# Five gate/up tiles in token halves that share a PSUM bank, a split block 0 down projection and new scheduler estimates, in a fused state-space and gated-MLP kernel

## The chip, the cores and the metric

The kernel runs on one core of a Trainium2 chip. The metric is device time in microseconds (us) of one execution. PE is TensorE, PEld its weight loads, DVE VectorE, ACT ScalarE, SP the engine that issues the DMAs. "L717" is line 717 of the kernel in question; the changed kernel has more lines, so the same statement has another number there.

## The reference, cut to what matters

```python
xn = layernorm(x)                                   # x: 2048 tokens x 512, bf16
A  = 2*Re(C @ scan(Lam_bar, B_bar @ xn)) + xn*Dskip # 512 complex states, scanned over tokens
B  = (gelu(xn @ w_gate) * (xn @ w_up)) @ w_down     # hidden size 1376
out = x + A + B
```

## The kernel before

The tokens are cut into 4 blocks of 512, and each block into 4 token tiles of 128. The hidden size is cut into 11 tiles ("ft"). For each block PE does gate/up (`GU`, 8 matmuls of 512 columns per hidden tile), the B projection of the scan (`BU`, 32 matmuls) and the down projection joined with the C projection (`DN`, 19 matmuls per token tile: 11 hidden parts, 8 state parts). The order on PE and SP is the program's. The order on DVE, ACT and POOL comes from a list scheduler, run when the kernel is built, which works with estimated durations:

```python
def d_pe(n_list):                                   # estimate of matmuls of n columns, ns
    return sum(max(n / 2.4 + 2.5, 64.0 + n / 4.7) for n in n_list)
```

At the start the normalized tokens of block 0 are transposed on PE and copied out of PSUM (where the results of PE land, in banks of 512 columns) by DVE or ACT, and three hidden tiles begin before all four token tiles are there:

```python
def TR0(j, eng):          # 4 transposes of token tile j, then a copy on DVE ("V") or ACT ("A")
    ...
def GU(b, fts=None, halves=False):
    ...
    if halves:
        for ft in fts:
            banks[ft] = (next_bank(), next_bank())          # gate bank, up bank
        def part(W, Wc, i, j0, j1):
            for ft in fts:
                mm(ft, W, Wc, banks[ft][i], 128 * j0, 128 * j1, XT0[j0:j1])
        part(WG, WGc, 0, 0, 1)      # gate, token tile 0: 12 matmuls of 128 columns
        part(WG, WGc, 0, 1, 2)      # gate, token tile 1
        part(WU, WUc, 1, 0, 2)      # up, token tiles 0 and 1: 12 of 256 columns
        TR0(2, "V")
        TR0(3, "A")
        part(WG, WGc, 0, 2, 3)
        part(WG, WGc, 0, 3, 4)
        part(WU, WUc, 1, 2, 4)
    for ft in fts:
        ...                         # other tiles: 8 matmuls of 512 columns
        # gelu (ACT) of the gate bank, copy (ACT) of the up bank, product (DVE)
```

```python
# order of the program (cut)
LN(0, [0, 1], True); TR0(0, "V"); TR0(1, "A"); fill(4); params()   # 4 filler matmuls
LN(0, [2, 3], True); load_B()
GU(0, [0, 1, 2], halves=True); tables_dve(); GU(0, [3, 4])
BU(0); CHAIN(0, 2); ...; GU(0, range(5, KF)); BU(1); ...
BU(2); CHAIN(2); DN(0); ...; DN(3)
```

`params()` puts some small operations on DVE (four to sixteen columns each). The weights come in three chunks each (hidden tiles 0 to 2, 3 to 6, 7 to 10); SP issues x tiles, gate chunk 0, up chunk 0, gate chunk 1, up chunk 1, and later the B transposes and chunk 2. Before all that, 11 warm-up matmuls run on PE.

Of the kernel before, what the change touches and what calls it, by code (L numbers as in the profile page):

```python
# [9 lines left out]
ALU = mybir.AluOpType  # L10
ACTF = mybir.ActivationFunctionType
# [2 lines left out]
ENGINES = ("tensor", "vector", "scalar", "gpsimd", "sync")  # L14
SYNC_LAT = 120.0
SELF_LAT = 40.0
DMA_ISSUE = 500.0
INORDER = ("tensor", "sync")

# [55 lines left out]
class Sched:  # L75
# [88 lines left out]
    def _backward(self, span):  # L164
        ops = self.ops
        left = {op.id: len(op.users) for op in ops}
        late = {op.id: span for op in ops}
        ready = {e: [] for e in ENGINES}
        last = {e: [op for op in ops if op.eng == e] for e in INORDER}
        for op in ops:  # L170
            if left[op.id] == 0 and op.eng not in INORDER:
                ready[op.eng].append(op)
        busy = {e: span for e in ENGINES}
        begin = {}
        n = len(ops)
        while n:
            best = None
            for e in ENGINES:
                if e in INORDER:
                    if not last[e] or left[last[e][-1].id]:  # L180
                        continue
                    op = last[e][-1]
                else:
                    if not ready[e]:
                        continue
                    op = max(ready[e], key=lambda o: (min(busy[e], late[o.id]), o.finish, o.id))
                end = late[op.id] if op.kind == "dma" else min(busy[e], late[op.id])
                if best is None or end > best[0]:
                    best = (end, op)
            end, op = best  # L190
            e = op.eng
            if e in INORDER:
                last[e].pop()
            else:
                ready[e].remove(op)
            begin[op.id] = end - op.dur
            if op.kind == "dma":
                begin[op.id] = min(begin[op.id], busy[e] - op.issue)
                busy[e] = begin[op.id]
            else:  # L200
                busy[e] = begin[op.id]
            n -= 1
            for d in op.deps:
                late[d.id] = min(late[d.id], begin[op.id] - (SELF_LAT if d.eng == op.eng and d.kind == "eng" else SYNC_LAT))
                left[d.id] -= 1
                if left[d.id] == 0 and d.eng not in INORDER:
                    ready[d.eng].append(d)
        return begin

    def _forward(self, prio):  # L210
        ops = self.ops
# [10 lines left out]
        nleft = len(ops)  # L222

        def rdy_time(op):
            return max([d.finish + (SELF_LAT if d.eng == op.eng and d.kind == "eng" else SYNC_LAT) for d in op.deps], default=0.0)

        while nleft:
            best = None
            for e in ENGINES:
                if e in INORDER:  # L230
                    if qpos[e] >= len(queue[e]):
                        continue
                    op = queue[e][qpos[e]]
# [3 lines left out]
                else:  # L237
# [4 lines left out]
                    stb, b = min(cands, key=lambda c: (prio[c[1].id], c[1].id))  # L242
# [107 lines left out]
EPS_BF16 = 1.0013580322265625e-05  # L350

def d_pe(n_list):
    return sum(max(n / 2.4 + 2.5, 64.0 + n / 4.7) for n in n_list)
def d_dve_tt2x(n): return 100.0 + 0.52 * n
def d_dve_1x(n): return 100.0 + 1.04 * n
def d_dve_scan(n): return 90.0 + 2.08 * n
# [2 lines left out]
def d_act(n, ptr=0): return 190.0 + 0.833 * n + 90.0 * ptr  # L359
# [3 lines left out]
def build(nc, ins, out):  # L363
    with ExitStack() as es:
# [151 lines left out]
        def next_bank():  # L516
            b_ = rstate["n"] % 8
            rstate["n"] += 1
            return b_
# [21 lines left out]

        w16 = lambda a, b_: W16.ap[:, a:b_]
        W16p = [A.sub(A.alloc("W16v", [4, 4], F32, at=W16.lo), "W16_%d" % i, i) for i in range(4)]
        GATE = {"before_gelu": []}
        sinT, sinP, cosT, cosP = (SC16.ap[:, 4 * i:4 * i + 4] for i in range(4))
        def coefs():
            V(lambda e: e.tensor_tensor(pa(LBR), pa(RRr), cosT, ALU.mult), D_TINY, [PA[RRr], SC16], [PA[LBR]])
# [155 lines left out]
            V(lambda e: e.tensor_tensor(ssb.ap[:, :, 1, :], TB.ap[:, :, 0, :], TA.ap[:, :, 1, :], ALU.subtract),  # L703
              d_dve_tt2x(2048), [TA, TB], [SSc[k3][s][1] for s in range(KP)], "post_im")

        def GU(b, fts=None, halves=False):
            k2 = b % 2
            fts = list(range(KF) if fts is None else fts)
            banks = {}

            def mm(ft, W, Wc, bank, c0, c1, rd):
                m = FROWS[ft]

                def f(e):
                    ins_ = None
                    for dk in range(KD):
                        ins_ = e.matmul(PS[bank][0:m, c0:c1], W.ap[:, dk, 128 * ft:128 * ft + m], XNT[b].ap[:, dk, c0:c1],  # L717
                                        start=(dk == 0), stop=(dk == KD - 1))
                    return ins_
                PE(f, d_pe([c1 - c0] * 4), [Wc[wchunk(ft)]] + rd, [BANK[bank]], "GU%d" % b)  # L720

            if halves:
                for ft in fts:
                    banks[ft] = (next_bank(), next_bank())
                def part(W, Wc, i, j0, j1):
                    for ft in fts:
                        mm(ft, W, Wc, banks[ft][i], 128 * j0, 128 * j1, XT0[j0:j1])
                part(WG, WGc, 0, 0, 1)
                part(WG, WGc, 0, 1, 2)
                part(WU, WUc, 1, 0, 2)  # L730
                TR0(2, "V")
                TR0(3, "A")
                part(WG, WGc, 0, 2, 3)
                part(WG, WGc, 0, 3, 4)
                part(WU, WUc, 1, 2, 4)
            for ft in fts:
                m = FROWS[ft]
                if not halves:
                    banks[ft] = (next_bank(), next_bank())
                bg, bu = banks[ft]  # L740
                kk = (KF * b + ft) % 3
                if not halves:
                    for (W, Wc, bank) in zip((WG, WU), (WGc, WUc), banks[ft]):
                        mm(ft, W, Wc, bank, 0, 512, XTr(b))
                GATE["last_gelu"] = ACT(lambda e, bg=bg, kk=kk, m=m: e.activation(  # L745
                    GG[kk].ap[0:m, :], PS[bg][0:m, :], ACTF.Gelu_apprx_tanh),
                    d_act(512), [BANK[bg]], [GG[kk]], "gelu", after=GATE["before_gelu"])
                ACT(lambda e, bu=bu, kk=kk, m=m: e.activation(UPB[kk].ap[0:m, :], PS[bu][0:m, :], ACTF.Copy),  # L748
                    d_act(512), [BANK[bu]], [UPB[kk]], "evU")
                V(lambda e, kk=kk, m=m, ft=ft, k2=k2: e.tensor_tensor(  # L750
                    HTt[k2][ft].ap[0:m, :], GG[kk].ap[0:m, :], UPB[kk].ap[0:m, :], ALU.mult),
                  d_dve_tt2x(512), [GG[kk], UPB[kk]], [HTt[k2][ft]], "hmul")

        def DN(b):
            k2, k3 = b % 2, b % 3
            for j in range(4):
                tt = 4 * b + j
                bank = next_bank()
                ko = tt % 4
                ACT(lambda e, bank=bank, tt=tt: e.activation(PS[bank][:, :], X[tt].ap, ACTF.Copy),  # L760
                    d_act(512), [X[tt]], [BANK[bank]], "seed")

                def f(e, bank=bank, j=j, k2=k2, k3=k3, b=b):
                    mms = []
                    for ft in range(KF):
                        m = FROWS[ft]
                        mms.append((PS[bank][:, :], HTt[k2][ft].ap[0:m, 128 * j:128 * (j + 1)], WD.ap[0:m, ft, :]))
                    for s in range(KP):
                        for c in range(2):
                            mms.append((PS[bank][:, :], SSc[k3][s][c].ap[:, 128 * j:128 * (j + 1)], CT[c][s].ap))  # L770
                    ins_ = None
                    for n, (o_, l_, r_) in enumerate(mms):
                        ins_ = e.matmul(o_, l_, r_, start=False, stop=(n == len(mms) - 1), skip_group_check=True)  # L773
                    return ins_
                rds = [HTt[k2][ft] for ft in range(KF)] + WDc
                rds += [SSs[k3][s] for s in range(KP)] + [CT[c][s] for c in range(2) for s in range(KP)]
                PE(f, d_pe([512] * (KF + 8)), rds + [BANK[bank]], [BANK[bank]], "DN%d" % b)
                V(lambda e, bank=bank, ko=ko, tt=tt: e.tensor_tensor(OUTB[ko].ap, PS[bank][:, :], XD[tt].ap, ALU.add),  # L778
                  d_dve_1x(512), [BANK[bank], XD[tt]], [OUTB[ko]], "evO")
                S.dma(lambda e, tt=tt, ko=ko: e.dma_start(out[0, 128 * tt:128 * (tt + 1), :], OUTB[ko].ap),  # L780
                      128 * 1024, reads=[OUTB[ko]], is_output=True, tag="st_out")

        nwarm = 11
        wrm4 = WRM.ap.unsqueeze(1).broadcast_to([128, 4, 128])
# [20 lines left out]
        params()  # L805
        LN(0, [2, 3], True)
        load_B()
        GU(0, [0, 1, 2], halves=True)
        tables_dve()
        GU(0, [3, 4])  # L810
        GATE["before_gelu"] = [tables_act([GATE["last_gelu"]])]
        BU(0)
        CHAIN(0, 2)
# [11 lines left out]
        GU(1, range(0, 8)); TR(2); GU(1, range(8, KF))  # L825
        BU(2)
        CHAIN(2)
        DN(0)
        LN(3); SKIP(3)
        GU(2, range(0, 8)); TR(3); GU(2, range(8, KF))  # L830
        BU(3)
# [62 lines left out]
```

## Time and profile before

| | before |
|---|---|
| time, median of 3 runs | 182.54 us (182.50 to 182.59) |
| span of the profiled run | 180.8 us |
| first gate matmul | 6.84 us |
| transposes of token tiles 2 and 3 | 9.49 us |
| next gate matmul | 10.82 us |
| first B matmul | 16.93 us |

The page of the kernel before, part 1 (busy time, share of the span, instructions) and the first line of part 4 (the chain of waits that ended last):

```profile
PE 175.2 (97%) x848; PEld 82.8 (46%) x864; DVE 155.8 (86%) x264; ACT 92.0 (51%) x158; POOL 7.5 (4%) x19
...
PE 95%; DVE 2%; issue 1%; ACT 0%; DVEq 0%
```

PE is the bound. How near to its limit it is cannot be read from busy time, because a matmul's recorded end is modelled (the Trainium skill, "Perfetto Trace Analysis", Tensor Engine Instruction, calls it an estimate; here a 512-column matmul is recorded as 379 ns while the next one starts 216 ns after it). So I go by the distance of starts. It is 216 ns for 512 columns, 109 for 256 and 56 for 128, from 10.82 us to the end, except where a record is missing.

The timeline of the kernel before, PE alone (start us, length us, line, shape, count, idle time before and its releaser):

```profile
5.80 0.72 PE L629 MATMUL PS<-arena 128*128 128x128 bf16 x8
6.36 0.39 PE L796 MATMUL PS<-arena 128*128 128x128 bf16 x4
...
6.84 2.81 PE L717 MATMUL PS<-arena 128*128 128x128 bf16 x36
9.49 0.61 PE L629 MATMUL PS<-arena 128*128 128x128 bf16 x8
10.82 6.28 PE L717 MATMUL PS<-arena 128*128 128x128 bf16 x51 [0.72 <-DVE arena L637]
16.93 0.38 PE L654 MATMUL PS<-arena 128*128 128x512 bf16 x1
```

The last transpose starts at 9.88 us, the next matmul 937 ns later, where 56 would do: 0.88 us are lost. DVE releases it. The timeline of the kernel before, DVE and then ACT, around the wait:

```profile
9.71 0.18 DVE L539 CAST arena<-arena 128x16 int32<-128x16 f32 x1
9.92 0.17 DVE L540 TENSOR_TENSOR arena<-arena 128x16 f32<-128x16 f32 x1
10.01 0.15 DVE L534 TENSOR_TENSOR arena<-arena 128x4 f32<-128x4 bf16 x1
10.08 0.15 DVE L552 TENSOR_TENSOR arena<-arena 128x4 f32<-128x4 f32 x1
10.27 0.18 DVE L553 RECIPROCAL arena<-arena 128x4 f32<-128x4 f32 x1
10.37 0.39 DVE L637 COPY arena<-PS 128x512 bf16<-128x512 bf16 x1
```

```profile
10.13 0.60 ACT L635 ACTIVATE arena<-PS 128x512 bf16<-128x512 bf16 x1 [2.06 <-PE PS L629]
```

L637 is the copy of token tile 2 on DVE. ACT copies tile 3 as soon as PE has transposed it. The chain of the kernel before, in order of time (start, length, what), runs through that copy:

```profile
10.45 0.32 DVE arena L637
10.77 0.05 issue
10.82 2.82 PE PS L717 x36
```

### The profile page before, as it was taken

To read this page: it belongs to the slowest core of one execution; us is meant where nothing else is said; L and a number is where in the kernel's file an instruction comes from. 1 tells how busy PE (TensorE), PEld (TensorE's weight loads), DVE (VectorE), ACT (ScalarE), POOL (GpSimd) and SP (SyncE) were. 2 spreads that over 40 slices of the span, in tenths; PEclk is the share of its full clock that TensorE was granted. 3 is DMA by queue.
4 is the path that set the end of the run, shared out by engine and by line. 5 is a ranking of instruction groups with operands and counts; after the bars stand their busy time and mean duration, and the time that the engine had idled before them with its cause. 6 is when DMAs were issued, how large, how long until landed. Compare 5 with 4: busy or idle time off the path is not lost.

```text
span 180.8 us, 2356 instructions
## 1 busy us (share of the span) xinstructions
PE 175.2 (97%) x848; PEld 82.8 (46%) x864; DVE 155.8 (86%) x264; ACT 92.0 (51%) x158; POOL 7.5 (4%) x19
## 2 busy tenths in 40 slices
PE   7989999999999999999999999999999999999993
PEld 2674444444444444444444444444444444444441
DVE  4899679999999996999999999999989999982111
ACT  3378999776767997002667793000667700800000
POOL 2220202000000002000000000000000000000000
PEclk9999999999999999999999999999999999999999
DMA  5999914999000000001610000000000000021100
GB/s 128 305 325 165 313 31 103 244 320 189 14 0 0 4 0 0 29 29 60 90 30 0 0 2 0 33 29 29 29 0 0 4 0 0 0 87 35 54 31 29
DMA packets 24068, 12.38 MB, mean 68 GB/s; under 512 B 15385, under 2 KB 24057, under 8 KB 24057
## 3 DMA queue, kind: packets, MB, share of 16 engines
q1 hardware_dynamic: 24032, 12.23, 28.2%
q8 instruction: 7, 0.11, 0.2%
q14 instruction: 5, 0.03, 0.1%
q10 hardware_dynamic: 24, 0.00, 0.0%
HBM read 6.46 MB, written 2.10 MB: 47 GB/s over the span
## 4 chain that ended last, share of the span: by engine, by line
PE 95%; DVE 2%; issue 1%; ACT 0%; DVEq 0%
PE PS L717 41%; PE PS L773 36%; PE PS L654 15%; PE PS L790 3%; DVE arena L637 0%; DVE arena L608 0%; DVE arena L778 0%; DVE arena L595 0%; PE PS L629 0%; ACT arena L599 0%; ACT arena L600 0%; DVE arena L539 0%; DVE arena L596 0%; DVE arena L538 0%; DVE arena L553 0%
## 5 line engine op out<-in xcount | busy, mean ns | idle before, releaser
L717 PE MATMUL PS<-arena 128*128 128x512 bf16 (+3 forms) x393 | 76.7, 353 | 1.1 <-DVE arena L637 0.7
L773 PE MATMUL PS<-arena 128*128 128x512 bf16 (+1 forms) x296 | 65.6, 379 | 0.4
L717 PEld LDWEIGHTS PS<-arena 128*128 128x128 bf16 (+1 forms) x400 | 37.8, 100 | 38.9 <-DVE arena L637 0.9
L745 ACT ACTIVATE arena<-PS 128x512 bf16<-128x512 f32 (+1 forms) x44 | 26.3, 599 | 49.1 <-PE PS L717 37.1
L773 PEld LDWEIGHTS PS<-arena 128*128 128x128 bf16 (+1 forms) x304 | 29.7, 98 | 36.0
L687 DVE TENSOR_TENSOR_SCAN arena<-arena 128x512 bf16<-128x512 f32 x32 | 38.6, 1251 | 0.0
L748 ACT ACTIVATE arena<-PS 128x512 bf16<-128x512 f32 (+1 forms) x44 | 26.3, 600 | 6.7 <-PE PS L717 6.6
L654 PE MATMUL PS<-arena 128*128 128x512 bf16 x127 | 28.2, 379 | 0.1
L778 DVE TENSOR_TENSOR arena<-PS,arena 128x512 bf16<-128x512 f32 x16 | 10.8, 684 | 15.5 <-PE PS L773 15.5
L654 PEld LDWEIGHTS PS<-arena 128*128 128x128 bf16 x128 | 12.5, 98 | 15.0
L658 ACT ACTIVATE arena<-PS 128x512 bf16<-128x512 f32 x32 | 17.8, 596 | 2.1 <-PE PS L654 2.1
L750 DVE TENSOR_TENSOR arena<-arena 128x512 bf16<-128x512 bf16 (+1 forms) x44 | 17.4, 415 | 0.8 <-ACT arena L748 0.8
L595 DVE BATCH_NORM_STATS2 arena<-arena 128x6 f32<-128x512 bf16 x16 | 10.2, 680 | 3.5 <-DMA arena<-in_A_x_dram 3.5
L760 ACT ACTIVATE PS<-arena 128x512 f32<-128x512 bf16 x16 | 9.4, 603 | 0.7
L674 DVE TENSOR_TENSOR arena<-arena 128x4096 bf16<-128x4096 bf16 (+1 forms) x5 | 9.3, 1859 | 0.0
L676 DVE TENSOR_TENSOR arena<-arena 128x4096 bf16<-128x4096 bf16 (+1 forms) x5 | 9.3, 1858 | 0.0
L699 DVE TENSOR_TENSOR arena<-arena 128x4096 bf16<-128x4096 bf16 x4 | 9.2, 2288 | 0.1
L700 DVE TENSOR_TENSOR arena<-arena 128x4096 bf16<-128x4096 bf16 x4 | 9.1, 2284 | 0.0
L608 DVE TENSOR_SCALAR arena<-arena 128x512 bf16<-128x512 bf16 x16 | 5.6, 409 | 0.3
L615 DVE TENSOR_TENSOR arena<-arena 128x512 bf16<-128x512 bf16 x16 | 5.8, 416 | 0.0
L790 PE MATMUL PS<-arena 128*128 128x512 bf16 x11 | 4.9, 632 | 1.0 <-DVE arena L508 1.0
L571 DVE SCALAR_TENSOR_TENSOR arena<-arena 128x512 bf16<-128x512 bf16 x8 | 5.6, 747 | 0.0
(75 smaller groups left out, 66.1 us busy)
## 6 DMA issues: line engine op xcount, KB each, us to landing
out_dram<-arena SPq DMA_DIRECT2D x16, 128.0 KB, 1.7
arena<-in_A_x_dram SPq DMA_DIRECT2D x3, 512.0 KB, 7.6
arena<-in_B_w_down_dram SPq DMA_DIRECT2D x1, 1280.0 KB, 8.2
arena<-in_A_x_dram SPq DMA_DIRECT2D x4, 128.0 KB, 2.2
arena<-in_B_w_gate_dram SPq DMA_DIRECT2D x1, 512.0 KB, 5.8
arena<-in_B_w_up_dram SPq DMA_DIRECT2D x1, 512.0 KB, 6.7
arena<-in_B_w_gate_dram SPq DMA_DIRECT2D x1, 480.0 KB, 4.6
arena<-in_B_w_up_dram SPq DMA_DIRECT2D x1, 480.0 KB, 6.0
```

The source lines that it names most:

```text
L595: V(lambda e, tt=tt: e.bn_stats(ST[tt].ap, X[tt].ap), d_dve_1x(512), [X[tt]], [ST[tt]], "bnst")
L654: ins_ = e.matmul(PS[bank][:, :], BBT[c][dk].ap[:, 128 * s:128 * (s + 1)], XNT[b].ap[:, dk, :], start=(dk == 0), stop=(dk == KD - 1))
L658: ACT(lambda e, bank=bank, k3=k3, s=s, c=c: e.activation(SSc[k3][s][c].ap, PS[bank][:, :], ACTF.Copy), d_act(512), [BANK[bank]], [SSc[k3][ ...
L687: V(lambda e, g=g, rb=rb, init=init: e.tensor_tensor_scan(g.ap, rb, g.ap, init, ALU.mult, ALU.add), d_dve_scan(512), [g, PA[RRr]] + ([CARc ...
L717: ins_ = e.matmul(PS[bank][0:m, c0:c1], W.ap[:, dk, 128 * ft:128 * ft + m], XNT[b].ap[:, dk, c0:c1], start=(dk == 0), stop=(dk == KD - 1))
L745: GATE["last_gelu"] = ACT(lambda e, bg=bg, kk=kk, m=m: e.activation(GG[kk].ap[0:m, :], PS[bg][0:m, :], ACTF.Gelu_apprx_tanh), d_act(512), ...
L748: ACT(lambda e, bu=bu, kk=kk, m=m: e.activation(UPB[kk].ap[0:m, :], PS[bu][0:m, :], ACTF.Copy), d_act(512), [BANK[bu]], [UPB[kk]], "evU")
L750: V(lambda e, kk=kk, m=m, ft=ft, k2=k2: e.tensor_tensor(HTt[k2][ft].ap[0:m, :], GG[kk].ap[0:m, :], UPB[kk].ap[0:m, :], ALU.mult), d_dve_tt ...
L760: ACT(lambda e, bank=bank, tt=tt: e.activation(PS[bank][:, :], X[tt].ap, ACTF.Copy), d_act(512), [X[tt]], [BANK[bank]], "seed")
L773: ins_ = e.matmul(o_, l_, r_, start=False, stop=(n == len(mms) - 1), skip_group_check=True)
L778: V(lambda e, bank=bank, ko=ko, tt=tt: e.tensor_tensor(OUTB[ko].ap, PS[bank][:, :], XD[tt].ap, ALU.add), d_dve_1x(512), [BANK[bank], XD[tt ...
L790: ins_ = e.matmul(PS[wb][:, :].rearrange("p (a b) -> p a b", a=4), WRM.ap, wrm4, start=True, stop=True)
```

## The change

The intent: let five hidden tiles begin with the first half of the tokens, so that more matmuls stand behind the transposes of tiles 2 and 3 while these are copied. The gate and up results of a token half (256 columns each) share one PSUM bank. In block 0's down projection all hidden parts come first, so that the state parts are wanted later. The scheduler's estimates change too.

```diff
+LAT = lambda d, op: SYNC_LAT if d.kind == "dma" or d.eng != op.eng else (0.0 if d.eng == "tensor" else SELF_LAT)
...                                  # used in both passes of the scheduler
 def d_pe(n_list):
-    return sum(max(n / 2.4 + 2.5, 64.0 + n / 4.7) for n in n_list)
+    return sum(n / 2.4 + 2.5 for n in n_list)
...
+        def GU_first(fts, early, single):
+            banks = [{ft: next_bank() for ft in fts} for h in range(2)]
+            ...     # mm: gate in columns 0-255 of the bank, up in 256-511; evac: gelu, copy, product of 256
+            for u in range(2):
+                for ft in early:
+                    mm(ft, u, 0, 1)          # gate, then up, token tile 0
+                ...
+            for ft in early:
+                for u in range(2):
+                    mm(ft, u, 1, 2)          # token tile 1
+                evac(ft, 0)
+            late = [ft for ft in fts if ft not in early]
+            mm(late[0], 0, 0, 2)
+            TR0(2, "V")
+            TR0(3, "A")
+            for ft in late[1:]:
+                mm(ft, 0, 0, 2)
+            for ft in late:
+                mm(ft, 1, 0, 2)
+                evac(ft, 0)
+            for ft in fts:
+                for u in range(2):
+                    mm(ft, u, 2, 4)
+                evac(ft, 1)
...
-        def DN(b):
+        def DN(b, split=False):
...
+            if split:
+                for j in range(4):
+                    seed(j); hidden(j)
+                for j in range(4):
+                    states(j); store(j)
...
-        GU(0, [0, 1, 2], halves=True)
+        GU_first(range(5), range(3), False)
         tables_dve()
-        GU(0, [3, 4])
...
-        DN(0)
+        DN(0, True)
```

Sharing a bank is sound. The Trainium skill ("PSUM — Partial Sum Buffer", The four PSUM rules) says that a group's first matmul clears the accumulate bits of the whole bank, so that two groups may not be open in one bank at once. Here each group of four matmuls is complete before the next starts in that bank.

More of the change, by code (lines that the diff above doesn't have):

```diff
@@ L203, in _backward @@
             for d in op.deps:
-                late[d.id] = min(late[d.id], begin[op.id] - (SELF_LAT if d.eng == op.eng and d.kind == "eng" else SYNC_LAT))
+                late[d.id] = min(late[d.id], begin[op.id] - LAT(d, op))
                 left[d.id] -= 1
@@ L224, in rdy_time @@
         def rdy_time(op):
-            return max([d.finish + (SELF_LAT if d.eng == op.eng and d.kind == "eng" else SYNC_LAT) for d in op.deps], default=0.0)
+            return max([d.finish + LAT(d, op) for d in op.deps], default=0.0)
         while nleft:
@@ L543, in build @@
         W16p = [A.sub(A.alloc("W16v", [4, 4], F32, at=W16.lo), "W16_%d" % i, i) for i in range(4)]
-        GATE = {"before_gelu": []}
+        GATE = {"before_gelu": [], "nh": 0}
         sinT, sinP, cosT, cosP = (SC16.ap[:, 4 * i:4 * i + 4] for i in range(4))
@@ L704, in CHAIN, with mm, f, evac @@
               d_dve_tt2x(2048), [TA, TB], [SSc[k3][s][1] for s in range(KP)], "post_im")
-        def GU(b, fts=None, halves=False):
+        def GU_first(fts, early, single):
+            banks = [{ft: next_bank() for ft in fts} for h in range(2)]
+            def mm(ft, u, j0, j1):
+                W, Wc = ((WG, WGc), (WU, WUc))[u]
+                h, q0 = j0 // 2, 256 * u + 128 * (j0 % 2)
+                bank = banks[h][ft]
+                def f(e):
+                    ins_ = None
+                    for dk in range(KD):
+                        ins_ = e.matmul(PS[bank][:, q0:q0 + 128 * (j1 - j0)], W.ap[:, dk, 128 * ft:128 * (ft + 1)],
+                                        XNT[0].ap[:, dk, 128 * j0:128 * j1], start=(dk == 0), stop=(dk == KD - 1))
+                    return ins_
+                PE(f, d_pe([128 * (j1 - j0)] * 4), [Wc[wchunk(ft)]] + XT0[j0:j1], [BANK[bank]], "GU0")
+            def evac(ft, h):
+                bank, c0 = banks[h][ft], 256 * h
+                GATE["nh"] = kk = (GATE["nh"] + 1) % 3
+                GATE["last_gelu"] = ACT(lambda e: e.activation(GG[kk].ap[:, 0:256], PS[bank][:, 0:256], ACTF.Gelu_apprx_tanh),
+                                        d_act(256), [BANK[bank]], [GG[kk]], "gelu")
+                ACT(lambda e: e.activation(UPB[kk].ap[:, 0:256], PS[bank][:, 256:512], ACTF.Copy),
+                    d_act(256), [BANK[bank]], [UPB[kk]], "evU")
+                V(lambda e: e.tensor_tensor(HTt[0][ft].ap[:, c0:c0 + 256], GG[kk].ap[:, 0:256], UPB[kk].ap[:, 0:256], ALU.mult),
+                  d_dve_tt2x(256), [GG[kk], UPB[kk]], [HTt[0][ft]], "hmul")
+            for u in range(2):
+                for ft in early:
+                    mm(ft, u, 0, 1)
+                if single and u == 0:
+                    TR0(1, "A")
+            for ft in early:
[15 more added lines that the diff above has]
+                evac(ft, 1)
@@ L707, in GU @@
+        def GU(b, fts=None):
             k2 = b % 2
@@ L720, in mm @@
                 PE(f, d_pe([c1 - c0] * 4), [Wc[wchunk(ft)]] + rd, [BANK[bank]], "GU%d" % b)
-            if halves:
-                for ft in fts:
-                    banks[ft] = (next_bank(), next_bank())
-                def part(W, Wc, i, j0, j1):
-                    for ft in fts:
-                        mm(ft, W, Wc, banks[ft][i], 128 * j0, 128 * j1, XT0[j0:j1])
-                part(WG, WGc, 0, 0, 1)
-                part(WG, WGc, 0, 1, 2)
-                part(WU, WUc, 1, 0, 2)
-                TR0(2, "V")
-                TR0(3, "A")
-                part(WG, WGc, 0, 2, 3)
-                part(WG, WGc, 0, 3, 4)
-                part(WU, WUc, 1, 2, 4)
             for ft in fts:
                 m = FROWS[ft]
-                if not halves:
-                    banks[ft] = (next_bank(), next_bank())
+                banks[ft] = (next_bank(), next_bank())
                 bg, bu = banks[ft]
                 kk = (KF * b + ft) % 3
-                if not halves:
-                    for (W, Wc, bank) in zip((WG, WU), (WGc, WUc), banks[ft]):
-                        mm(ft, W, Wc, bank, 0, 512, XTr(b))
+                for (W, Wc, bank) in zip((WG, WU), (WGc, WUc), banks[ft]):
+                    mm(ft, W, Wc, bank, 0, 512, XTr(b))
                 GATE["last_gelu"] = ACT(lambda e, bg=bg, kk=kk, m=m: e.activation(
@@ L752, in GU @@
                   d_dve_tt2x(512), [GG[kk], UPB[kk]], [HTt[k2][ft]], "hmul")
-        def DN(b):
+        def DN(b, split=False):
             k2, k3 = b % 2, b % 3
-            for j in range(4):
-                tt = 4 * b + j
-                bank = next_bank()
-                ko = tt % 4
-                ACT(lambda e, bank=bank, tt=tt: e.activation(PS[bank][:, :], X[tt].ap, ACTF.Copy),
-                    d_act(512), [X[tt]], [BANK[bank]], "seed")
-                def f(e, bank=bank, j=j, k2=k2, k3=k3, b=b):
-                    mms = []
-                    for ft in range(KF):
-                        m = FROWS[ft]
-                        mms.append((PS[bank][:, :], HTt[k2][ft].ap[0:m, 128 * j:128 * (j + 1)], WD.ap[0:m, ft, :]))
-                    for s in range(KP):
-                        for c in range(2):
-                            mms.append((PS[bank][:, :], SSc[k3][s][c].ap[:, 128 * j:128 * (j + 1)], CT[c][s].ap))
-                    ins_ = None
-                    for n, (o_, l_, r_) in enumerate(mms):
-                        ins_ = e.matmul(o_, l_, r_, start=False, stop=(n == len(mms) - 1), skip_group_check=True)
-                    return ins_
-                rds = [HTt[k2][ft] for ft in range(KF)] + WDc
-                rds += [SSs[k3][s] for s in range(KP)] + [CT[c][s] for c in range(2) for s in range(KP)]
-                PE(f, d_pe([512] * (KF + 8)), rds + [BANK[bank]], [BANK[bank]], "DN%d" % b)
-                V(lambda e, bank=bank, ko=ko, tt=tt: e.tensor_tensor(OUTB[ko].ap, PS[bank][:, :], XD[tt].ap, ALU.add),
@@ new lines, in DN, with seed, mms, f @@
+            banks = [next_bank() for _ in range(4)]
+            def seed(j):
+                tt, bank = 4 * b + j, banks[j]
+                ACT(lambda e: e.activation(PS[bank][:, :], X[tt].ap, ACTF.Copy), d_act(512), [X[tt]], [BANK[bank]], "seed")
+            def mms(j, ops, last, rds):
+                bank = banks[j]
+                def f(e):
+                    ins_ = None
+                    for n, (l_, r_) in enumerate(ops):
+                        ins_ = e.matmul(PS[bank][:, :], l_[:, 128 * j:128 * (j + 1)], r_, start=False,
+                                        stop=last and n == len(ops) - 1, skip_group_check=True)
+                    return ins_
+                PE(f, d_pe([512] * len(ops)), rds + [BANK[bank]], [BANK[bank]], "DN%d" % b)
@@ new lines, in hidden, with states, store @@
+            def hidden(j):
+                ops = [(HTt[k2][ft].ap[0:FROWS[ft], :], WD.ap[0:FROWS[ft], ft, :]) for ft in range(KF)]
+                mms(j, ops, False, [HTt[k2][ft] for ft in range(KF)] + WDc)
+            def states(j):
+                ops = [(SSc[k3][s][c].ap, CT[c][s].ap) for s in range(KP) for c in range(2)]
+                mms(j, ops, True, [SSs[k3][s] for s in range(KP)] + [CT[c][s] for c in range(2) for s in range(KP)])
+            def store(j):
+                tt, bank = 4 * b + j, banks[j]
+                ko = tt % 4
+                V(lambda e: e.tensor_tensor(OUTB[ko].ap, PS[bank][:, :], XD[tt].ap, ALU.add),
@@ L779, in DN @@
                   d_dve_1x(512), [BANK[bank], XD[tt]], [OUTB[ko]], "evO")
-                S.dma(lambda e, tt=tt, ko=ko: e.dma_start(out[0, 128 * tt:128 * (tt + 1), :], OUTB[ko].ap),
+                S.dma(lambda e: e.dma_start(out[0, 128 * tt:128 * (tt + 1), :], OUTB[ko].ap),
                       128 * 1024, reads=[OUTB[ko]], is_output=True, tag="st_out")
+            if split:
[3 more added lines that the diff above has]
+                    states(j); store(j)
+            else:
+                for j in range(4):
+                    seed(j); hidden(j); states(j); store(j)
```

## The prediction

> **What bounds the kernel now.** TensorE. The chain of waits that ended last is 95% PE; after warm-up the waits view shows one wait of PE (0.7 us). From 10.81 us to the last matmul at 177.7 us PE runs back to back: starts of 128x512 matmuls lie 216 ns apart, 128x256 109 ns, 128x128 56 ns (timeline), the N/2.4 + 2.5 ns of the Trainium skill ("TensorE: Matmul & The Clock Gate", Back-to-back issue gap). 784 matmuls of 512 columns, or their equal, are 169 of 180.8 us. So only idle time of PE can be won: in the start, or the 3 us tail, which the change does not touch.
>
> **The idle time at stake.** Gate/up work of three tiles runs 6.84 to 9.49 us (token tiles 0 and 1), the transposes of tiles 2 and 3 to 9.93, then PE stands until 10.81 for the evictions of these transposes (VectorE until 10.76, ScalarE until 10.73). Starts are 937 ns apart where 56 would do: 0.88 us lost, on the critical path.
>
> **What the change moves.** With five tiles open in token halves, gate and up sharing a bank, 12 matmuls of 256 columns (12 x 109 = 1.3 us) stand behind the transposes, whose evictions land within about 1.1 us: -0.88 us.
>
> New cost 1: up weights are wanted after 12 matmuls (6.84 + 0.67 = 7.51 us) instead of at 8.18. The DMA list has that chunk issued at 3.13 and landing 4.6 us later, 7.71: a new wait of 0.2 to 0.3 us. The second chunk's gate weights land at 9.48 (wanted about 9.8), its up weights at 10.93 (wanted about 11.1): just in time.
>
> New cost 2: 16 matmuls of 512 columns become 32 of 256: 16 x (2 x 109.1 - 216) = 0.04 us.
>
> Off the path: 20 activations of 256 columns for 10 of 512 (estimated from their 0.49 us spacing at some 0.3 us: 6 us where ScalarE has 8).
>
> The block 0 down projection has no wait of PE before it: the last scaled C tile is ready at 65.3 us, the state parts at 60.0, it starts at 67.2. Hidden parts first (44 x 216 ns = 9.5 us) buy slack, no time. The scheduler constants reorder VectorE and ScalarE; I expect no stall from it.
>
> The first B matmuls move from 16.93 to about 16.4 us; their transpose lands at 15.69, in time. The third weight chunk lands by 21.8 us, wanted at 23.3.
>
> **Sum.** -0.88 + 0.27 + 0.04 = -0.57 us: 182.54 becomes **182.0 us**, range 181.6 to 182.5. Chances: faster by over 2% 0.005, within 2% 0.985, slower by over 2% 0.01.
>
> **What would show it.** PE's timeline: no gap near 10 us; a gap of 0.2 to 0.3 us near 7.5 us, ended by the up weights' DMA; the first B matmul near 16.4 us; 216 ns spacing to the end; first down-projection matmul near 66.6 us without a wait; tail 3 us.
>
> **What would make it wrong.** ScalarE may put gelu evictions ahead of the copy of transpose 3, and the wait comes back (up to 0.9 us). The new list schedule may delay a step that frees a bank or feeds a later block: VectorE is busy all the time from 35 to 67 us. If the up weights land earlier, the gain is up to 0.84 us; if the B transpose lands after 16.4 us, it is lost there.

## The result, and the profile after

| | before | after |
|---|---|---|
| median of 4 runs | 182.52 us (182.48 to 182.59) | 182.48 us (182.07 to 182.76) |
| ratio | | 0.9996 (95%: 0.9973 to 1.0018) |
| span of the profiled run | 180.8 us | 180.3 us (that run took 182.07) |

The surprise is the spread: 0.69 us in four runs, where the kernel before had 0.11. The profiled run happened to be the fastest.

The page of the changed kernel, the lines that answer to those of before:

```profile
PE 175.4 (97%) x865; PEld 84.7 (47%) x880; DVE 156.0 (87%) x269; ACT 93.5 (52%) x168; POOL 9.5 (5%) x19
...
PE 97%; issue 1%; DVE 0%; DVEq 0%
```

The timeline of the changed kernel, PE alone:

```profile
5.75 1.03 PE L630 MATMUL PS<-arena 128*128 128x128 bf16 x8
6.58 0.45 PE L845 MATMUL PS<-arena 128*128 128x128 bf16 x4
...
7.06 3.29 PE L718 MATMUL PS<-arena 128*128 128x128 bf16 x52
10.19 0.61 PE L630 MATMUL PS<-arena 128*128 128x128 bf16 x8
10.64 5.95 PE L718 MATMUL PS<-arena 128*128 128x256 bf16 x52
16.64 0.59 PE L655 MATMUL PS<-arena 128*128 128x512 bf16 x2
```

The wait after the transposes is gone: matmuls follow at 10.64 us, and the two copies run behind them. (The first B matmul's record is missing: 16.64 lies one matmul too late, so the B work starts at 16.42.) DVE's copy of tile 2 and ACT's copy of tile 3 in the timeline of the changed kernel:

```profile
10.70 0.42 DVE L638 COPY arena<-PS 128x512 bf16<-128x512 bf16 x1
```

```profile
10.84 0.60 ACT L636 ACTIVATE arena<-PS 128x512 bf16<-128x512 bf16 x1
```

The chain of the changed kernel stays on PE through the same stretch, which is new:

```profile
7.13 3.22 PE PS L718 x52
10.35 0.45 PE PS L630 x8
10.80 5.78 PE PS L718 x52
```

In this profile the sum reads so. The wait goes: -0.88 us. The first gate matmul is 0.22 later (7.06 against 6.84), because PE was still at half speed: the transposes and fillers start 107 ns apart until 6.75 us, against 56 from about 6.0 us before. One matmul waits 0.10 us at 11.17 us for the second chunk of up weights, which landed at 11.12. The smaller matmuls cost 0.04. Together -0.52, and the first B matmul moved by -0.51 (16.93 to 16.42). The weight-load row of the waits view of the changed kernel names that DMA (total, times, longest, us):

```profile
PEld PS L718 <- DMA arena<-in_B_w_up_dram: 0.2, 1, 0.2
```

From the first B matmul on nothing differs. The last matmul starts 160.43 us after it in the kernel before, in the changed kernel and in all twelve profiles told below (where the first B matmul's record is missing, it is taken 0.216 us earlier). All that is to be explained lies in the first 17 us.

### The profile page after: what moved, and what is told of

Read it like the earlier page. It is cut to its first block, busy times and chain, and to the rows that moved or that the text cites. A ratio compares the mean times of both kernels' runs of the same rounds, so it can differ in the third digit from the quotient of the medians.

```text
span 180.3 us, 2405 instructions
## 1 busy us (share of the span) xinstructions
PE 175.4 (97%) x865; PEld 84.7 (47%) x880; DVE 156.0 (87%) x269; ACT 93.5 (52%) x168; POOL 9.5 (5%) x19
## 4 chain that ended last, share of the span: by engine, by line
PE 97%; issue 1%; DVE 0%; DVEq 0%
PE PS L767 37%; PE PS L802 36%; PE PS L655 15%; PE PS L718 5%; PE PS L839 3%; PE PS L630 1%; DVE arena L818 0%; PE PS L845 0%; DVE arena L505 0%; PE PS L530 0%; DVEq L331 0%; DVE arena L509 0%
## 5 line engine op out<-in xcount | busy, mean ns | idle before, releaser
L767 PE MATMUL PS<-arena 128*128 128x512 bf16 (+1 forms) x308 | 67.8, 379 | 0.2
L802 PE MATMUL PS<-arena 128*128 128x512 bf16 (+1 forms) x297 | 65.8, 379 | 0.4
L767 PEld LDWEIGHTS PS<-arena 128*128 128x128 bf16 (+1 forms) x312 | 31.3, 100 | 36.1
L779 ACT ACTIVATE arena<-PS 128x512 bf16<-128x512 f32 (+1 forms) x39 | 23.5, 602 | 45.6 <-PE PS L767 36.4
L802 PEld LDWEIGHTS PS<-arena 128*128 128x128 bf16 (+1 forms) x304 | 29.7, 98 | 36.0
L655 PE MATMUL PS<-arena 128*128 128x512 bf16 x124 | 27.7, 379 | 0.2
L782 ACT ACTIVATE arena<-PS 128x512 bf16<-128x512 f32 (+1 forms) x39 | 23.4, 601 | 6.9 <-PE PS L767 6.8
L655 PEld LDWEIGHTS PS<-arena 128*128 128x128 bf16 x128 | 12.5, 98 | 14.8
L784 DVE TENSOR_TENSOR arena<-arena 128x512 bf16<-128x512 bf16 (+1 forms) x39 | 15.4, 415 | 1.2 <-ACT arena L782 1.0
L718 PE MATMUL PS<-arena 128*128 128x256 bf16 (+1 forms) x104 | 9.2, 248 | 0.0
L718 PEld LDWEIGHTS PS<-arena 128*128 128x128 bf16 x104 | 8.0, 98 | 0.8 <-DMA arena<-in_B_w_up_dram 0.2
L839 PE MATMUL PS<-arena 128*128 128x512 bf16 x11 | 4.9, 632 | 1.0 <-DVE arena L509 1.0
```

What stands on the lines that cost most here:

```text
L655: ins_ = e.matmul(PS[bank][:, :], BBT[c][dk].ap[:, 128 * s:128 * (s + 1)], XNT[b].ap[:, dk, :], start=(dk == 0), stop=(dk == KD - 1))
L718: ins_ = e.matmul(PS[bank][:, q0:q0 + 128 * (j1 - j0)], W.ap[:, dk, 128 * ft:128 * (ft + 1)], XNT[0].ap[:, dk, 128 * j0:128 * j1], start=( ...
L767: ins_ = e.matmul(PS[bank][0:m, c0:c1], W.ap[:, dk, 128 * ft:128 * ft + m], XNT[b].ap[:, dk, c0:c1], start=(dk == 0), stop=(dk == KD - 1))
L779: GATE["last_gelu"] = ACT(lambda e, bg=bg, kk=kk, m=m: e.activation(GG[kk].ap[0:m, :], PS[bg][0:m, :], ACTF.Gelu_apprx_tanh), d_act(512), ...
L782: ACT(lambda e, bu=bu, kk=kk, m=m: e.activation(UPB[kk].ap[0:m, :], PS[bu][0:m, :], ACTF.Copy), d_act(512), [BANK[bu]], [UPB[kk]], "evU")
L784: V(lambda e, kk=kk, m=m, ft=ft, k2=k2: e.tensor_tensor(HTt[k2][ft].ap[0:m, :], GG[kk].ap[0:m, :], UPB[kk].ap[0:m, :], ALU.mult), d_dve_tt ...
```

## The experiments

Twelve labels ran, ten of them other kernels and two the changed kernel again, in three groups; the kernels of a group share a chip and the runs of the kernel before. All gave correct results.

| kernel | group | runs | mean us | range us | before, mean | ratio (95%) |
|---|---|---|---|---|---|---|
| again (changed kernel) | 1 | 6 | 182.14 | 181.80 to 182.59 | 182.63 | 0.9974 (0.9961 to 0.9986) |
| first_only | 1 | 5 | 182.15 | 181.83 to 182.53 | 182.63 | 0.9974 (0.9962 to 0.9986) |
| all_but_first | 1 | 5 | 182.24 | 182.15 to 182.42 | 182.63 | 0.9979 (0.9967 to 0.9991) |
| small_chunk | 1 | 5 | 181.98 | 181.67 to 182.14 | 182.63 | 0.9963 (0.9950 to 0.9976) |
| dpe_only | 2 | 5 | 182.28 | 182.10 to 182.51 | 182.58 | 0.9980 (0.9966 to 0.9993) |
| first_oldconst | 2 | 5 | 182.41 | 182.13 to 182.71 | 182.58 | 0.9990 (0.9978 to 1.0003) |
| small_no_fill | 2 | 5 | 181.91 | 181.64 to 182.25 | 182.58 | 0.9963 (0.9950 to 0.9976) |
| look_after (changed kernel) | 2 | 2 | 181.94 | 181.75 to 182.14 | 182.58 | 0.9965 (0.9946 to 0.9983) |
| late_up | 3 | 5 | 181.85 | 181.74 to 182.00 | 182.75 | 0.9951 (0.9938 to 0.9964) |
| late_small_no_fill | 3 | 6 | 181.77 | 181.59 to 182.03 | 182.75 | 0.9947 (0.9932 to 0.9961) |
| cold_after | 3 | 2 | 183.57 | 183.49 to 183.66 | 182.75 | 1.0045 (1.0024 to 1.0066) |
| cold_before | 3 | 2 | 184.23 | 183.70 to 184.76 | 182.75 | 1.0081 (1.0051 to 1.0112) |

### again: is the spread real?

The changed kernel unchanged. My first theory blamed the clock: PE leaves half speed at a moment that differs from run to run, and the old wait had hidden this. The rivals were late weights of the second chunk, and a late B transpose.

> The changed kernel unchanged, to see its spread. Its four runs lay at 182.07, 182.26, 182.70 and 182.76 us where the kernel before stays within 182.48 to 182.59. Theory clock: TensorE leaves half speed[...]; before hid up to 0.88 us of it in its wait, the changed kernel has no wait left, so the time is spread over some 0.7 us and follows that moment, 0.5 us for each us of half speed after 5.8 us. Rival weights: the second up-weight chunk (landing 11.12 us, PE waits 0.10 us for it) lands later in slow runs, and the wait at 11.2 us grows by what the run is slower. Rival B: the B transpose (landing 15.8) comes after 16.4 us in slow runs. All expect a spread of some 0.7 us again; if the runs now agree within 0.15 us, none of them.

Measured: 181.80 to 182.59 us, so the spread is real, and the mean is 0.49 us under before. With the first four runs and the two of look_after, the twelve runs of the changed kernel have a mean of 182.21 and a range of 181.75 to 182.76; the 24 runs of before in the same rounds have 182.59 and 182.44 to 182.83. So the change gains about 0.38 us (182.59 - 182.21), less than predicted and more than the first four runs showed. The size is loose: by group the means differ by 0.08, 0.49 and 0.64 us.

### first_only: is the split down projection worth anything?

```diff
-        DN(0, True)
+        DN(0)
```

> The changed kernel with the block 0 down projection as before (hidden and state parts in one). Main theory: no wait stood before that projection, so the split is worth 0: same mean as the changed kernel within 0.15 us, same spread. Rival: without the split the new order opens a wait of PE near 67 us, 0.2 us or more slower.

Measured: ratio 0.9974, the same as the changed kernel in the same rounds. No wait of PE opens later in its profile. The split is worth nothing here. Its profiled run was the slowest of its five (182.53): the first x tile landed 0.5 us later than in the other profiles (3.29 us against 2.73 to 2.95), and the first transposes with it (6.25 us). The first up weights were late too (8.26), and PE waited 0.17 us for them.

### all_but_first: the change without its main part

The kernel before, with the split projection and the new scheduler estimates, but the old three tiles.

```diff
-        GU_first(range(5), range(3), False)
+        GU(0, [0, 1, 2], halves=True)
         tables_dve()
+        GU(0, [3, 4])
```

> The kernel before with the split down projection and the scheduler constants, without the five tiles in halves. Main theory: the 0.88 us wait near 10 us stays and hides the clock's phase: 182.5 us with a spread of 0.15 us or less, like before. Rival (the spread comes from the new order of VectorE and ScalarE later on): spread of 0.4 us or more.

Measured: it missed my expectation. The ratio is 0.9979, so it gains 0.39 us without the five tiles. In its profile the wait near 10 us is 0.46 us, where it was 0.88. The order on DVE had changed: the copy of tile 2 came ahead of five of the parameter operations.

### dpe_only: one line of the scheduler

To see which line did that, I changed only the estimate of a matmul's duration in the kernel before. The order on PE is unchanged.

```diff
-    return sum(max(n / 2.4 + 2.5, 64.0 + n / 4.7) for n in n_list)
+    return sum(n / 2.4 + 2.5 for n in n_list)
```

> The kernel before with one line changed: the scheduler's estimate of a matmul (n / 2.4 + 2.5 without the floor of 64 + n / 4.7). It makes VectorE copy the transpose of token tile 2 ahead of five small parameter operations. Theory estimate: this line alone shrinks the 0.88 us wait near 10 us to about 0.46 us, as it did with all but the first part changed, and the mean falls by 0.4 us (ratio 0.998). Rival (the gain of that run came from the split projection or the latency constant): the wait stays at 0.88 us and the ratio is 1.000.

The timelines of dpe_only, PE and then DVE:

```profile
9.76 0.61 PE L629 MATMUL PS<-arena 128*128 128x128 bf16 x8
10.67 6.28 PE L717 MATMUL PS<-arena 128*128 128x128 bf16 x51 [0.30 <-DVE arena L637]
```

```profile
9.66 0.17 DVE L538 TENSOR_SCALAR arena<-arena 128x8 f32<-128x8 f32 x1
10.18 0.43 DVE L637 COPY arena<-PS 128x512 bf16<-128x512 bf16 x1 [0.35 <-PE PS L629]
```

DVE now waits for PE (0.35 us) instead of the other way round, and the wait of PE is 0.46 us by starts. Ratio 0.9980. One line of a build-time estimate gives most of what the whole change gives (0.30 of about 0.38 us, two means whose intervals overlap). The latency rule was not tried alone; with it and the split, all_but_first has the same ratio (0.9979).

### first_oldconst: the five tiles with the old estimates

The changed kernel with `d_pe`, the latency rule and the down projection as before:

```diff
-    return sum(n / 2.4 + 2.5 for n in n_list)
+    return sum(max(n / 2.4 + 2.5, 64.0 + n / 4.7) for n in n_list)
...
-        DN(0, True)
+        DN(0)
```

> The five tiles in halves with the old scheduler constants and the old down projection. Theory: VectorE's copy comes late again behind the parameter operations, but 1.3 us of matmuls stand behind the transposes, so PE does not wait near 10 us: same time as the changed kernel (ratio 0.997 to 0.9985, runs spread over 0.5 us or more). Rival: the new constants are needed, and a PE wait of 0.3 us or more returns near 12 us.

PE does not wait near 10 to 12 us in its profile: the 1.3 us of matmuls behind the transposes are enough, even with the late copy. That was expected. The ratio of 0.9990 came out just above the range that I gave, with an interval that overlaps it, so its size is unclear. Its profile shows what makes such a run slow. The timeline of first_oldconst, PE alone:

```profile
7.42 0.84 PE L717 MATMUL PS<-arena 128*128 128x128 bf16 x12 [0.51 <-DMA arena<-in_B_w_gate_dram]
8.51 2.62 PE L717 MATMUL PS<-arena 128*128 128x128 bf16 x40 [0.25 <-DMA arena<-in_B_w_up_dram]
```

PE waits for the first chunk of gate weights (landed 7.37 us, against 6.62 in the profile of before) and then for the first chunk of up weights (8.46 against 7.71). This profile was at full speed from 4.7 us on, earlier than most, and yet it is the slowest run of its five (182.71). The clock cannot be the cause of it.

### look_after: another look at the changed kernel

> The changed kernel again, for one more point of time against the moment of full speed. Theory clock plus start: the first B matmul starts at (first transpose) + 10.1 us + 0.5 us for each us between the first transpose and the moment of full speed + waits for weights, within 0.1 us (it held so in the two profiles: 16.42 and 16.26 us measured, with 5.75 us and full speed at 6.68 and 6.58 us).

The timeline of look_after, PE alone, and then its chain of waits (start, length, what):

```profile
6.86 0.84 PE L718 MATMUL PS<-arena 128*128 128x128 bf16 x12
7.93 2.62 PE L718 MATMUL PS<-arena 128*128 128x128 bf16 x40 [0.23 <-DMA arena<-in_B_w_up_dram]
10.39 0.61 PE L630 MATMUL PS<-arena 128*128 128x128 bf16 x8
```

```profile
3.14 4.75 DMA arena<-in_B_w_up_dram
7.89 0.05 issue
7.93 2.62 PE PS L718 x40
```

Full speed came at 4.2 us, before any useful matmul, and still this run (182.14) was slower than the profiled run of again (181.88, full speed at 6.64). It waited 0.40 us for the first chunk of up weights (7.93 - 6.86, less 12 x 56 ns), and the chain now comes from that DMA and not from PE. The expectation itself missed: it gives 16.28 us for the first B matmul (5.78 + 10.1 + 0.40), which came at 16.51, and 0.1 us was allowed. My clock theory, as the cause of the spread, falls.

The profiles of the normally warmed kernels that have the five tiles and want the up weights after 12 matmuls give, together, the rule. "Expected" is the larger of (up weights landed + 2.50) and (first gate matmul + 3.13), where 2.50 and 3.13 us are the matmuls that lie between, at 56 and 109 ns, with some 0.05 us of signalling behind a DMA. "Full speed from" is read from the spacing of starts; the profile's clock record puts it up to 0.15 us earlier (6.68 and 6.58 in the first two):

| profile | full speed from | up weights landed | first gate matmul | wait for up weights | second transposes | expected |
|---|---|---|---|---|---|---|
| after (first profile) | 6.75 | 7.47 | 7.06 | 0 | 10.19 | 10.19 |
| again | 6.64 | 7.32 | 7.01 | 0 | 10.14 | 10.14 |
| small_chunk | 7.0 | 7.88 | 7.23 | 0 | 10.38 | 10.38 |
| look_after | 4.2 | 7.89 | 6.86 | 0.40 | 10.39 | 10.39 |
| small_no_fill | 6.6 | 8.02 | 6.97 | 0.41 | 10.52 | 10.52 |
| first_only | 6.9 | 8.26 | 7.47 | 0.17 | 10.76 | 10.76 |
| first_oldconst | 4.7 | 8.46 | 7.42 | 0.41 | 10.97 | 10.96 |

Half speed and late weights are not added up; the later one counts. (The rule takes it that PE is at full speed by about the first gate matmul: in cold_after, below, it gives 10.56 and the transposes came at 11.64.) In each of the seven the run's time is this start plus 171.73 to 171.77 us, or 171.88 in the first, which has the 0.10 us wait. So the start explains these runs. They are of five kernels, though, and only three of the changed one (181.88 to 182.14 us): its slower runs, up to 182.76, have no profile, and that late weights made them slow is inferred, not shown. In these seven profiles the first up chunk landed between 7.32 and 8.46 us, and the start of the second transposes spread over 0.83 us with it. Before, the up weights were wanted only at 8.18 us, and a wait of 0.88 us stood behind. So in the kernel before the same landings had up to 0.67 us more room (8.18 - 7.51), and a wait behind them that hid some of the rest.

### small_chunk: are the second chunk's weights the cause?

```diff
-FCH = [(0, 384), (384, 896), (896, F)]
+FCH = [(0, 384), (384, 640), (640, 896), (896, F)]   # the third and fourth load after the B transposes
```

> The changed kernel with the second weight chunk cut to the two tiles that GU_first needs (256 KB each in place of 512), the rest loaded after the B transposes. The up weights of tiles 3 and 4 should land near 9.5 us in place of 11.1. Theory clock: the 0.10 us wait at 11.2 us goes, the mean falls by 0.1 us and the spread of 0.7 us stays. Rival weights: the spread shrinks to 0.2 us and the mean falls by 0.3 us or more. Rival B: the B transposes start about 1 us earlier, so the spread shrinks too, with no wait at 16.4 us.

The second chunk's up weights landed at 9.56 us in place of 11.12, and the wait of 0.10 us near 11.2 is gone. The spread was 0.47 us, between the 0.7 and the 0.2 of the theories. The mean is 0.16 us under the changed kernel in the same rounds, with overlapping intervals. The rival "second chunk" explains 0.10 us at most; it was the wrong chunk. The rival "B transpose" finds no support: in no profile did the first B matmul wait.

### small_no_fill: without the fillers

The smaller chunk of small_chunk, and:

```diff
-        fill(4)
```

> Smaller second weight chunk and no four filler matmuls ahead of the first gate matmuls. In the changed kernel PE is on the path from 5.75 us on, and the fillers cost 4 x 107 ns at half speed or 4 x 56 at full. Theory clock: first gate matmuls start 0.15 to 0.2 us earlier (then the copy of token tile 0 bounds), mean 0.1 us or more under the changed kernel and 0.6 us under before. Rival: the fillers keep the clock up or the up weights bound, so nothing is gained (within 0.05 us of the smaller chunk alone).

Ratio 0.9963, equal to small_chunk's in the other group, so nothing is shown to be gained. The profile says why in that run: the first gate matmul, at 6.97 us, itself followed its weights (landed at 6.92), and PE then waited 0.41 us for up weights that landed at 8.02.

### late_up: ask for the up weights later

The rule suggests a remedy: the three early tiles' gate matmuls for both token tiles go first, then the up matmuls (as 12 of 256 columns), so that the up weights are wanted after 24 small matmuls and not after 12.

```diff
-            for u in range(2):
+            for j in range(2):
                 for ft in early:
-                    mm(ft, u, 0, 1)
-                if single and u == 0:
-                    TR0(1, "A")
+                    mm(ft, 0, j, j + 1)
             for ft in early:
-                for u in range(2):
-                    mm(ft, u, 1, 2)
+                mm(ft, 1, 0, 2)
                 evac(ft, 0)
```

> The changed kernel with the first three tiles' gate matmuls for token tiles 0 and 1 ahead of their up matmuls (12 of 256 columns), so that the up weights are wanted after 24 small matmuls instead of 12, about 0.67 us later. Theory: of the two start-up costs the larger one counts, half speed or up weights. The wait for the up weights (0.40 us where the clock came up early and they landed at 7.9, 0.41 at 8.0, 0 where it came up at 6.6 to 7) should be 0 for landings up to about 8.1 us: mean 0.1 to 0.3 us under the changed kernel, 182.0 or less. Rival (the clock alone makes the spread): same mean within 0.05 us.

The timeline of late_up, PE alone:

```profile
7.06 3.25 PE L718 MATMUL PS<-arena 128*128 128x128 bf16 x40
10.15 0.61 PE L630 MATMUL PS<-arena 128*128 128x128 bf16 x8
...
16.38 0.81 PE L655 MATMUL PS<-arena 128*128 128x512 bf16 x3
```

The up weights landed at 8.00 us in this profile, which would have put the changed kernel's second transposes at 10.50 by the rule; here they start at 10.15, without a wait. The five runs lie within 0.26 us, where twelve of the changed kernel spread over 1.01. The mean is 181.85, 0.90 us under before in the same rounds, against 0.49 and 0.64 for the changed kernel in its two groups. These are different groups, and the intervals of the ratios overlap slightly (up to 0.9964 here, from 0.9961 in again), so the times alone show neither the size of the step nor quite its sign; the missing wait is in the run itself. The spread is a weak measure too: it is five runs against twelve, and the kernel before, which spread over 0.39 us in 24 runs, spread over 0.64 in the eleven of this group (182.49 to 183.13).

### late_small_no_fill: all remedies together

The edits of late_up, small_chunk and small_no_fill in one kernel.

> The later up matmuls, the smaller second weight chunk and no fillers together. Theory: no wait for weights but the first chunk of gate weights (landing 6.2 to 7.4 us) and half speed stay; gate matmuls start about 6.75 us. Mean about 181.75 us, 0.8 us under the kernel before, ratio 0.9955. Rival: the next bound (copy of token tile 0, first gate weights) eats it, mean 182.0 as with smaller chunk alone.

Mean 181.77 us, ratio 0.9947: the fastest kernel, 0.98 us under before. The mean is as predicted within 0.02 us, but the lead over before was to be 0.8 us: before was slower in this group, so the close hit is partly luck. Its lead over late_up (0.08 us) is inside the intervals, so I don't call the other two parts gains. In its profile no matmul waits for weights, the second transposes start at 9.99 and the first B matmul at 16.11.

### cold_after and cold_before: what half speed costs

One warm-up matmul in place of 11; every other engine keeps its order.

```diff
-        nwarm = 11
+        nwarm = 1
```

> The changed kernel with 1 warm-up matmul in place of 11, all else in the same order: full speed should come 3 to 6 us after the first transposes, at 8.8 to 11.8 us. Theory clock: with no wait left to hide it each us of half speed costs 0.5: first B matmul at 5.75 + 10.1 + 0.5 x (moment of full speed - 5.75), within 0.2 us, 17.4 to 18.9 us, and 183.0 to 184.5 us in all. Rival (half speed costs nothing here, weights bound): first B matmul at 16.4 to 16.8 us as ever.

> The kernel before with 1 warm-up matmul in place of 11. Theory: the first 0.44 us of a later second transpose are hidden, because VectorE copies it only after its parameter operations; first B matmul at 16.93 - 0.44 + 0.5 x (moment of full speed - 5.8) within 0.25 us. Rival (before hides the whole 0.88 us): 0.44 us earlier than that. Rival (before hides nothing): 0.44 us later.

The timeline of cold_before, PE alone:

```profile
7.42 4.85 PE L717 MATMUL PS<-arena 128*128 128x128 bf16 x36
12.11 0.61 PE L629 MATMUL PS<-arena 128*128 128x128 bf16 x8
13.02 6.28 PE L717 MATMUL PS<-arena 128*128 128x128 bf16 x52 [0.29 <-DVE arena L637]
```

The timeline of cold_before, DVE, its copy of token tile 2:

```profile
12.54 0.42 DVE L637 COPY arena<-PS 128x512 bf16<-128x512 bf16 x1 [1.81 <-PE PS L629]
```

In cold_after full speed came at 9.9 us and the first B matmul at 17.77; the formula gives 17.9, within the 0.2 us allowed. Its second transposes moved by 1.45 us (10.19 to 11.64) and its last matmul by 1.35: the rest is the 0.10 us for the second up chunk, which was no longer awaited. So the changed kernel hides nothing of PE's own delays.

In cold_before full speed came at 11.7 us and the first B matmul at 19.13. The formula gave 19.43, so it missed by 0.30 us, beyond the 0.25 allowed; by this number alone the rival that the whole 0.88 is hidden (18.99) lies nearer. Why the formula missed is not shown. The direct reading needs no formula: the second transposes moved by 2.62 us (9.49 to 12.11), the matmul behind the wait by 2.20 (10.82 to 13.02). So the old wait hid 0.42 us, close to the 0.44 expected, and not the whole 0.88. In before DVE came to its copy that much late, behind the parameter operations. In cold_before it was done with these and waited 1.81 us for PE; the 0.46 us of wait that stay (13.02 less 12.11, less 8 x 56 ns) are the copy itself, as in dpe_only and all_but_first, where DVE also waited for PE.

Half speed is therefore real as a cost, but small in normal runs: it puts the first gate matmul at 7.0 to 7.2 us in place of 6.86 (after, again, small_chunk against look_after, whose gate weights landed only at 6.81; before has 6.84 at full speed). The Trainium skill ("TensorE: Matmul & The Clock Gate", What's actually happening) says that the activity window which lifts the throttle is free-running, so that the moment varies. The profiles agree that it varies, but by more than the 500 ns either way that the page gives: full speed came between 4.2 and 7.0 us with the same warm-up, and at 4.2 and 6.75 in two executions of one kernel (look_after and after).

## Why the prediction was right or wrong

The median of the first four runs, 182.48 us, lies just inside the range of 181.6 to 182.5. The mean of twelve runs, 182.21, lies nearer to the 182.0 predicted. The mechanism held: the wait went, and nothing moved later. Of the sum's costs one term was mis-sized and others were missing. That the first profile came so close (-0.51 us against -0.57) is partly luck: 0.22 and 0.10 us that I had not forecast stand where 0.27 was forecast and nothing paid.

- **The wait of 0.88 us goes: right.** No profile with five tiles has it. It was not all the change's to win, though. I wrote that the scheduler constants would bring no stall, and did not see that they would bring a gain. One of them halves the same wait (0.88 to 0.46 us) and alone gives a ratio of 0.9980, so that what the five tiles add beyond it is not clear of the noise (0.9979 without them and 0.9974 with them in one group; 0.9990, up to 1.0003, for the five tiles with the old estimates).
- **"New cost 1", the up weights, 0.27 us: the term that was mis-sized.** I worked out 7.71 (landed) less 7.51 (wanted) from one trace and entered it as a constant. It measured 0 in three of the profiles above, 0.17 in one and 0.40 to 0.41 in three, because the landing moves between 7.32 and 8.46 us from run to run. It is also not independent of the clock.
- **A term was missing: half speed at the start.** It put the first gate matmul 0.22 us later in the first profile. Before, up to 0.42 us of such a delay was hidden by the wait that the change takes away; I treated the start at 6.84 us as fixed.
- **The second chunk "just in time": nearly.** 0.10 us in the first profile and in late_up, none in again or look_after.
- **Smaller matmuls, 0.04 us; the split projection, 0; no stall later: right.** The first down-projection matmul starts at 66.49 us (66.6 forecast) without a wait. The 160.43 us from the first B matmul to the last matmul are the same everywhere.

What stays open: why the DMAs of the first chunks land up to 1.1 us (up) and 1.3 us (gate, 6.10 to 7.37) apart from run to run (not the chip alone: on the chip of group 1 the up chunk landed at 7.32 to 8.26), and how the remaining spread of late_up divides between the gate weights, the x tiles and the clock. No kernel took the variation of the landings away, so the cause of the landings themselves was not tried.

## What to carry to other kernels

A wait that is taken away had been a buffer: list what could arrive late behind it (weights, clock, inputs) and how much later each is wanted in the new order, before the whole wait is booked as a gain. When a kernel's spread grows after such a change, look at slow runs' profiles too, and not only at the one that happens to be fast. And when a build-time scheduler orders the engines, test its constants alone: here one estimate reordered DVE, where one copy mattered, and alone gave 0.30 us, where the whole change gave about 0.38.

## What the Trainium skill lacked or had wrong

- "TensorE: Matmul & The Clock Gate", Back-to-back issue gap: it gives 81 ns for 128 columns and 131 ns for 512 as the sustained spacing in a real kernel with weight loads. Here every matmul has its own weight load, and the spacing is 56 and 216 ns, which is what the same section gives for the isolated case.
- The same page, PE-mode transpose: it says that full speed does not engage for transposes. In the kernel before, the transposes of token tiles 2 and 3 start 56 ns apart, the same as matmuls of 128 columns, at full clock. Whether transposes count as activity is not shown here.
- "DMA: Bandwidth & Descriptors": it has no figure for how far the landing of one and the same load moves from run to run. Here the first 384 KB up chunk, issued at 3.12 to 3.14 us each time, landed between 7.32 and 8.46 us in the profiles.
